# A recurrent layer and a gated convolution in one kernel: the written-out order of all queues is replaced by another order of the same operations

## The chip, the cores and the metric

The kernel runs on one core of a Trainium2 chip. The metric is the device time of one execution, in microseconds (us), smaller is better. Times are medians of several runs; a profile comes from one further, profiled execution.

## The reference, cut to what matters

The inputs `x`, `r_gate` and `i_gate` have 4 sequences of 6336 steps with 256 channels each, in fp32. First comes a gated linear recurrence along each sequence:

```
log_a = 8 * sigmoid(r_gate) * log(clip(sigmoid(a_param), 1e-6, 1 - 1e-6))
a     = exp(log_a)
u     = sqrt(max(1 - a*a, 1e-6)) * sigmoid(i_gate) * x
h[t]  = a[t] * h[t-1] + u[t];   y[t] = h[t]          # per sequence and channel
```

Then comes a gated unit on `y`: a causal convolution of 5 taps for each channel, a sigmoid of it, and two 256x256 products:

```
gate = sigmoid(sum_k conv_w[k] * y[t-4+k])
out  = (gate * (y @ w_val)) @ w_out
```

## The kernel before, in words

The four sequences lie one behind the other as 25344 rows. They are cut into 50 load **windows** (49 of 512 rows, the last of 256), numbered w, and into 27 **chunks**, numbered c: chunk 0 is window 0, chunk 1 is window 1, chunks 2 to 24 are two windows each (chunk c is windows 2c-2 and 2c-1), chunks 25 and 26 are windows 48 and 49. On the output side the last window is two windows of 128 rows, 49 and 50. The halves of the 256 channels are h = 0 and 1.

There is no loop over the work. A string `ORDER` lists some 900 words, one for each operation, and a loop at the end of the kernel (L588) calls the function of each word. Every engine takes its own instructions in the order of the words, one after the other, and waits at its next one until that one's inputs are there and its output place is free. So the string fixes five queues at once, and the numbers behind `@` in a word say which of the eight PSUM banks it uses. The words, with engine and line of the profile:

| word | engine | what it does |
|---|---|---|
| `lr.w`, `li.w`, `lx.w` | SP, L292 | DMA load of a window of r_gate, i_gate, x (512 KB each) into rings of 4 windows |
| `st.w` | SP, L562 | DMA store of an output window (512 KB) from a ring of 4 |
| `ta.c`, `tb.c` | ACT, L310, L313 | tanh of r_gate and i_gate (frees the load's place) |
| `tr.c.h` | PE, L357 | transposes of the r part into PSUM |
| `ex.c.h` | ACT, L373 | a = exp(...) into `aring`, for two chunks at once |
| `sq.c.h`, `sa.c.h` | POOL L381, ACT L389 | a*a; the one or the other engine, by word |
| `rt.b.k` | ACT, L406 | square root, for two chunks at once; needs a table load (L578) before and behind |
| `rd.0.0` | DVE, L419 to L427 | the root of chunk 0 in eight arithmetic steps |
| `nt.c` | PE, L441 | transposes of the root into PSUM |
| `pp.w`, `up.w` | POOL, L320, L332 | (tanh + 1), and its product with x into `uring` |
| `xp.w`, `uv.w` | PE L337, DVE L346 | the same product for five windows near the start, with x passed through PSUM |
| `xg.c` | DVE, L452, L456 | product with the root |
| `xt.c.h` | PE, L466 | transposes of it into PSUM |
| `sc.c.h` | DVE, L499 | the recurrence as a scan, into `yring` |
| `cv.w` | PE, L511 | convolution, 20 products with diagonals |
| `tg.w` | ACT, L518 | tanh of it into `tgring` |
| `vl.w` | PE, L526 | y @ w_val |
| `gv.w` | DVE, L531 | gate times value |
| `ou.w.0` | PE, L541 | product with w_out |
| `cd.w.0`, `ca.w.0` | DVE L549, ACT L551 | copy from PSUM to `oring`; the one or the other engine, by word |
| `s_...` | several | set-up: identity, constants from `a_param`, the diagonals, the weights |

A chunk goes through loads, `ta`, `tr`, `ex`, `sq`, `rt` (four chunks, in two pieces, between two table loads), `nt`, `xg`, `xt`, `sc`, and then each of its windows through `cv`, `tg`, `vl`, `gv`, `ou`, a copy and `st`. A load of window w waits until the operation that read window w-4 from the same ring is through. SP issues loads and stores from one queue: a store whose copy is not done yet holds every load behind it.

Of the kernel before, what the change touches and what calls it, by code (L numbers as in the profile page):

```python
# [49 lines left out]
xt.1.1@6 xt.2.1@0 sc.1.1 tg.0 li.9 sc.2.1 li.8 ex.4.1 vl.0@4,5 xt.2.0@1 tr.4.0@6,7 tb.4 gv.0 sq.5.1 cv.1@2,3 sc.2.0  # L50
ex.4.0 li.11 pp.5 lx.7 xp.4@4,5 lx.6 pp.6 uv.4 ta.6 pp.7 nt.3@6,7 up.5 ou.0.0@0,1 ta.7 lr.14 cv.3@4,5 cd.0.0 li.10
sq.5.0 lx.9 xg.3 tg.3 cv.2@0,1 lr.15 tg.1 lx.8 st.0 vl.1@6,7 sq.4.1 tg.2 xt.3.1@4 gv.1 tb.5 tr.6.0@0,1 sc.3.1 up.7
tr.6.1@6,7 ex.6.0 vl.2@2,3 up.6 lx.11 gv.2 li.12 ou.1.0@4,5 ex.6.1 lr.17 cd.1.0 xt.3.0@2 lr.16 sq.4.0 lx.10 sc.3.0
li.13 tb.6 ou.2.0@6,7 sq.7.0 vl.3@0,1 ta.8 li.15 cv.4@4,5 gv.3 sq.6.1 cd.2.0 tg.4 lr.18 ou.3.0@2,3 cd.3.0 sq.7.1
xp.8@0,1 lx.12 uv.8 rt.3.0 li.14 vl.4@2,3 st.1 sq.6.0 gv.4 lr.19 xp.9@6,7 uv.9 pp.11 lx.13 ou.4.0@2,3 rt.3.1 pp.10
cd.4.0 st.2 nt.4@6,7 up.10 xg.4 nt.5@0,1 xg.5 xt.4.0@4 up.11 lx.14 sc.4.0 xt.5.0@3 nt.6@6,7 tb.7 xt.4.1@2 sc.4.1
vl.5@0,1 ta.9 cv.5@4,5 li.16 pp.12 pp.13 xg.6 tg.5 lr.21 up.12 lr.20 tb.8 gv.5 li.17 tr.8.0@6,7 lx.15 sc.5.0 xt.6.1@0
up.13 lx.16 ex.8.0 xt.5.1@1 li.18 li.19 tr.8.1@4,5 sc.5.1 nt.7@2,3 pp.14 ex.8.1 st.3 ou.5.0@6,7 sq.9.0 st.4 ta.10 xg.7
cv.8@4,5 lx.17 up.14 cd.5.0 cv.6@2,3 tg.8 sc.6.1 xt.6.0@1 tg.6 pp.15 vl.6@4,5 ta.11 cv.7@2,3 sq.8.1 gv.6 cv.9@6,7 tg.7
lr.24 sc.6.0 up.15 lr.25 tb.9 st.5 ou.6.0@2,3 lr.23 tr.10.0@4,5 sq.8.0 cd.6.0 tg.9 vl.7@0,1 ex.10.0 st.6 gv.7 vl.8@2,3  # L60
lx.19 pp.16 xt.7.1@6 li.20 gv.8 xt.7.0@7 sq.9.1 tb.10 tr.10.1@0,1 sc.7.1 ou.7.0@4,5 sq.11.0 ex.10.1 cv.10@2,3 li.23
cd.7.0 tg.10 cv.11@0,1 sq.11.1 sc.7.0 st.7 ta.13 lr.22 lx.18 ou.8.0@4,5 li.21 pp.17 li.22 vl.9@2,3 tg.11 cd.8.0 sq.10.1
lr.29 gv.9 vl.11@4,5 sq.10.0 st.8 rt.4.0 gv.11 vl.10@0,1 ou.9.0@6,7 gv.10 up.17 cd.9.0 ou.10.0@0,1 rt.4.1 cd.10.0 up.16
ou.11.0@6,7 cd.11.0 st.10 nt.8@2,3 lr.28 pp.19 lx.21 xg.8 nt.9@0,1 lx.20 pp.18 xg.9 xt.8.1@3 cv.12@6,7 up.18 sc.8.1
ta.12 xt.8.0@5 up.19 tg.12 lr.26 sc.8.0 nt.10@2,3 lr.27 tb.11 st.9 tr.12.1@6,7 xt.9.1@1 xg.10 cv.14@4,5 ex.12.1 li.24
pp.20 li.25 sc.9.1 lx.22 pp.21 vl.14@2,3 lx.23 tg.14 cv.13@6,7 sq.13.1 tb.12 gv.14 vl.12@4,5 up.21 gv.12 tg.13
# [43 lines left out]
def kernel(  # L110
# [80 lines left out]
    with tc.manual_schedule():  # L191
# [187 lines left out]
        def op_sq(c, h):  # L379
            e, a = squares(c, h)  # L380
            nc.gpsimd.tensor_tensor(out=e, in0=a, in1=a, op=ALU.mult)  # L381
# [228 lines left out]
```

## Time and profile before

| what | value |
|---|---|
| median of 3 runs | 281.95 us (281.42 to 282.34) |
| profiled execution, span from the first to the last instruction | 279.6 us |
| around the span (median less span) | 2.4 us |
| PE, DVE, ACT, POOL busy | 243.8, 258.2, 267.0, 233.0 us |
| moved by DMA | 104.75 MB, 375 GB/s on average |

The profiled execution has no time of its own beside its span; the median of the runs less that span, 2.4 us, is taken for what lies around it.

How to read the profile: a row of the view of groups names the line, the engine, the operation, output and inputs, the shape and the count, then the busy time, the mean of one in ns, and the engine's idle time just ahead of these instructions with what ended it. A row of the timeline gives start and duration in us; `x2` behind it are two instructions that follow each other. A row of the view of windows gives, for a stretch of time, its length, the busy time and count of instructions of each engine, the clock that TensorE was granted (1.00 is full), the busy share of the 16 DMA engines and the rate at which they moved data. A row of the view of waits gives the total, the number and the longest of the waits of one line for another.

### The profile page before, as it was taken

How to read it: one execution, taken by the hardware profiler on the slowest of the kernel's cores; microseconds unless marked ns; L12 is line 12 of the kernel's file. 1: busy time of each engine (PE TensorE's matmuls, PEld its weight loads, DVE VectorE, ACT ScalarE, POOL GpSimd, SP SyncE). 2: the span in 40 equal slices, each digit the busy share in tenths (PEclk: the TensorE clock that was granted, in tenths of full speed). 3: DMA queues.
4: the chain of work that ended last, by engine and by line, in shares of the span. 5: the costliest groups of instructions: out<-in, count | busy, mean ns of one | idle time of the engine just before them, and what ended most of it. 6: DMA issues, size and time to landing. Idle time of an engine off the chain costs nothing. (4 is left out here: it accounts for less than half of the span.)

```text
span 279.6 us, 6233 instructions
## 1 busy us (share of the span) xinstructions
PE 243.8 (87%) x2493; PEld 164.9 (59%) x2493; DVE 258.2 (92%) x221; ACT 267.0 (96%) x187; POOL 233.0 (83%) x152
## 2 busy tenths in 40 slices
PE   2368999898799779999889999899999899999994
PEld 2143566456647466874566575666675756856563
DVE  5587797899999999899999999999999999999992
ACT  5999999999999999999999999999999999999754
POOL 1569679997999998999999999999999977984200
PEclk9998899999999999999999999999999999999999
DMA  7999999999999999999999999999999999742765
GB/s 275 411 405 385 388 409 409 413 409 409 419 408 417 415 414 416 413 416 409 420 413 341 415 420 414 414 411 420 416 363 407 420 378 400 286 176 92 283 263 194
DMA packets 29563, 104.75 MB, mean 375 GB/s; under 512 B 3287, under 2 KB 4062, under 8 KB 29534
## 3 DMA queue, kind: packets, MB, share of 16 engines
q1 hardware_dynamic: 29520, 104.35, 94.4%
q8 instruction: 19, 0.31, 0.4%
q14 instruction: 10, 0.08, 0.1%
q10 hardware_dynamic: 14, 0.01, 0.0%
HBM read 78.39 MB, written 25.95 MB: 373 GB/s over the span
## 5 line engine op out<-in xcount | busy, mean ns | idle before, releaser
L381 POOL TENSOR_TENSOR ering<-aring 128x1024 f32<-128x1024 f32 (+1 forms) x51 | 90.7, 1799 | 13.8 <-ACT aring L373 13.7
L332 POOL TENSOR_TENSOR uring<-tbring,xring 128x1024 bf16<-128x1024 bf16 (+1 forms) x45 | 95.5, 2139 | 3.2 <-DMA xring<-in_x_dram 1.7
L499 DVE TENSOR_TENSOR_SCAN yring<-aring,yring,banks 128x1024 bf16<-128x1024 f32 (+4 forms) x46 | 96.8, 2116 | 0.8 <-PE banks L466 0.7
L511 PE MATMUL banks<-yring,diag 64*64 64x512 bf16 (+6 forms) x1080 | 63.1, 362 | 3.8 <-ACT aring L373 1.1
L531 DVE SCALAR_TENSOR_TENSOR tgring<-tgring,banks 128x1024 bf16<-128x1024 bf16 (+1 forms) x51 | 59.4, 1178 | 6.1 <-PE banks L526 5.1
L320 POOL TENSOR_SCALAR tbring<-tbring 128x1024 bf16<-128x1024 bf16 (+1 forms) x45 | 46.3, 1040 | 10.3 <-ACT tbring L313 10.3
L541 PE MATMUL banks<-wo,tgring 128*128 128x256 bf16 x396 | 50.9, 273 | 4.4 <-DVE tgring L531 2.1
L373 ACT ACTIVATE aring<-banks,khf 128x2048 f32<-128x2048 bf16 (+3 forms) x32 | 52.9, 1689 | 0.2 <-PE banks L357 0.2
L526 PE MATMUL banks<-yring,wv 128*128 128x512 bf16 (+4 forms) x216 | 50.1, 361 | 2.7 <-DVE oring L549 1.0
L518 ACT ACTIVATE tgring<-banks 128x1024 bf16<-128x1024 f32 (+1 forms) x51 | 50.6, 1011 | 0.8 <-PE banks L511 0.6
L541 PEld LDWEIGHTS <-tgring 128*128 128x128 bf16 x396 | 42.3, 114 | 14.2 <-DVE tgring L531 5.8
L310 ACT ACTIVATE taring<-rring 128x2048 bf16<-128x2048 f32 (+2 forms) x27 | 47.9, 1785 | 1.7 <-DMA rring<-in_r_gate_dram 1.7
L313 ACT ACTIVATE tbring<-iring 128x2048 bf16<-128x2048 f32 (+2 forms) x27 | 48.1, 1782 | 0.0
L511 PEld LDWEIGHTS <-diag 64*64 64x64 bf16 x1080 | 29.4, 105 | 27.7 <-issue 12.5
L406 ACT ACTIVATE ering<-ering 128x4096 bf16<-128x4096 f32 (+3 forms) x14 | 43.6, 3157 | 0.1
L549 DVE COPY oring<-banks 128x1024 f32<-128x1024 f32 (+1 forms) x34 | 39.9, 1189 | 0.4 <-PE banks L541 0.4
L357 PE MATMUL banks<-ident_b,taring 128*128 128x128 bf16 x396 | 29.4, 230 | 8.5 <-ACT taring L310 4.5
L466 PE MATMUL banks<-ident,uring 128*128 128x128 f32 x198 | 30.3, 279 | 4.4 <-DVE uring L452 1.6
L357 PEld LDWEIGHTS <-taring 128*128 128x128 bf16 x396 | 26.0, 103 | 12.3 <-issue 6.3
L526 PEld LDWEIGHTS <-wv 128*128 128x128 bf16 x216 | 19.1, 97 | 23.8 <-issue 10.2
L466 PEld LDWEIGHTS banks<-ident,uring 128*128 128x128 f32 x198 | 21.9, 141 | 14.5 <-DVE uring L452 3.4
L441 PEld LDWEIGHTS banks<-ident,ering 128*128 128x128 f32 x184 | 24.2, 208 | 6.8 <-issue 3.0
(52 smaller groups left out, 160.0 us busy)
## 6 DMA issues: line engine op xcount, KB each, us to landing
rring<-in_r_gate_dram SPq DMA_DIRECT2D x49, 512.0 KB, 8.4
iring<-in_i_gate_dram SPq DMA_DIRECT2D x49, 512.0 KB, 9.0
xring<-in_x_dram SPq DMA_DIRECT2D x49, 512.0 KB, 9.4
out_dram<-oring SPq DMA_DIRECT2D x49, 512.0 KB, 9.0
oring<-in_moe_w_val_dram SPq DMA_DIRECT2D x1, 256.0 KB, 8.9
rring<-in_r_gate_dram SPq DMA_DIRECT2D x1, 256.0 KB
iring<-in_i_gate_dram SPq DMA_DIRECT2D x1, 256.0 KB, 6.5
xring<-in_x_dram SPq DMA_DIRECT2D x1, 256.0 KB
```

The costliest lines, as they stand in the source:

```text
L313: nc.scalar.activation(**tangent(c, tbring, NTI, iring, NII))
L332: nc.gpsimd.tensor_tensor(out=u, in0=t1, in1=xt, op=ALU.mult)
L357: nc.tensor.transpose(out=bank[:, o:o + P], in_=taring[:, place(w, NTR), j, h * P:(h + 1) * P], identity=ident_b[:])
L373: nc.scalar.activation(out=dst, in_=src, func=ACT.Exp, scale=khf[:, h:h + 1], bias=khf[:, h:h + 1])
L381: nc.gpsimd.tensor_tensor(out=e, in0=a, in1=a, op=ALU.mult)
L466: nc.tensor.transpose(out=out[:, o + q:o + wins[w] // 2:nq], in_=uring[:, w % NU, q, h * P:(h + 1) * P, :].rearrange("p d two -> p (d two) ...
L499: nc.vector.tensor_tensor_scan(out=yring[:, h, col:col + o1 - o0], data0=aring[:, h, a_at[c] + o0:a_at[c] + o1], data1=xT[:, o0:o1], initi ...
L511: nc.tensor.matmul(out=gp[oh * 64:oh * 64 + 64, h, a:b], lhsT=diag[half * 64:half * 64 + 64, h, k, :], rhs=yring[half * 64:half * 64 + 64, ...
L518: nc.scalar.activation(out=tgring[:, w % NTG, :, 0:outs[w]], in_=live.pop(("gp", w))[:, :, 0:outs[w]], func=ACT.Tanh, scale=0.5)
L526: nc.tensor.matmul(out=val[:, m, a:b], lhsT=wv[:, hk, m * P:(m + 1) * P], rhs=yring[:, hk, col:col + b - a], start=(hk == 0), stop=(hk == ...
L531: nc.vector.scalar_tensor_tensor(out=tgring[:, w % NTG, :, 0:outs[w]], in0=tgring[:, w % NTG, :, 0:outs[w]], scalar=1.0, in1=live.pop(("va ...
L541: nc.tensor.matmul(out=ops[:, j * D:(j + 1) * D], lhsT=gv[:, hk, j:outs[w]:J], rhs=wo[:, hk, :], start=(hk == 0), stop=(hk == H - 1))
```

## The change

The string `ORDER` is another one. The functions that the words call and the rings that they use do the same as before. Counted by words, the work is the same but for these:

- The copy of window 20 moves from ACT (`ca.20.0`) to DVE (`cd.20.0`). At the end, `cd.49.0 ca.50.0` becomes `ca.49.0 cd.50.0`.
- Of the squares, `sa.21.1` on ACT becomes `sa.20.1`, and `sa.26.0` and `sa.26.1` (256 columns each) go from ACT to POOL.
- The set-up words `s_kt` and `s_diag` are split into their PE and DVE parts, `s_ktp s_ktd` and `s_dgp s_dgc s_dgd`. `op_vl` accepts a single bank for the last two short windows. Three new functions (`op_pq`, `op_uq`, `op_sb`) are called by no word.

All else is where a word stands, and its banks. The queues in the first part of the run, taken from the two strings (the first line of each pair is before, the second after):

```
DVE  rd.0.0 uv.0 xg.0 sc.0.0 sc.0.1 xg.1 uv.2 sc.1.0 xg.2 sc.1.1 sc.2.1 gv.0 sc.2.0 uv.4 cd.0 xg.3 gv.1 sc.3.1 gv.2 cd.1 sc.3.0 gv.3 cd.2 cd.3 uv.8 gv.4 uv.9 cd.4 xg.4 xg.5
DVE  rd.0.0 uv.0 xg.0 uv.2 sc.0.0 sc.0.1 xg.1 sc.1.0 xg.2 sc.1.1 sc.2.0 uv.4 sc.2.1 gv.0 xg.3 cd.0 gv.2 gv.1 sc.3.1 cd.2 sc.3.0 gv.3 cd.1 cd.3 gv.4 uv.9 uv.8 cd.4 xg.4 xg.5

PE   tr.2.1 tr.2.0 xp.0 nt.0 xt.0.0 nt.1 xt.0.1 xp.2 nt.2 xt.1.0 cv.0 tr.4.1 xt.1.1 xt.2.1 vl.0 xt.2.0 tr.4.0 cv.1 xp.4 nt.3 ou.0.0
PE   tr.2.1 tr.2.0 xp.0 nt.0 xp.2 xt.0.0 xt.0.1 nt.1 xt.1.0 nt.2 xt.1.1 cv.0 xt.2.0 tr.4.1 xp.4 tr.4.0 xt.2.1 vl.0 cv.1 nt.3 cv.2 ou.0.0

ACT  ta.6 ta.7 tg.3 tg.1 tg.2 tb.5 ex.6.0 ex.6.1 tb.6 ta.8 tg.4 rt.3.0 rt.3.1 tb.7 ta.9 tg.5
ACT  tg.1 tb.4 tg.2 ta.6 ta.7 tg.3 tb.5 ex.6.1 ex.6.0 tb.6 tg.4 rt.3.0 rt.3.1 tb.7 tg.5 ta.8 ta.9

SP   lx.7 lx.6 lr.14 li.10 lx.9 lr.15 lx.8 st.0 lx.11 li.12 lr.17 lr.16 lx.10 li.13 li.15 lr.18 lx.12 li.14 st.1 lr.19 lx.13 st.2
SP   lx.7 li.9 li.8 lx.6 st.0 li.10 li.11 lr.16 lx.9 st.2 lx.8 lx.10 st.1 li.12 li.13 st.3 lr.15 lr.14 lx.11 st.4 lr.17
```

Two further places, DVE around chunk 8 and the end of SP's queue:

```
DVE  cd.9 cd.10 cd.11 xg.8 xg.9 sc.8.1 sc.8.0 xg.10
DVE  cd.11 cd.9 xg.8 sc.8.1 xg.9 sc.8.0 sc.9.1

SP   li.49 li.48 st.37 lx.47 lx.48 st.38 st.40 lx.49 st.39 st.42 ...
SP   li.49 lx.46 st.37 lx.48 li.48 lx.49 lx.47 st.39 st.38 st.40 ...
```

Of the diff itself, the head and the end of the string and the code that changes:

```diff
-s_ident s_small s_kt s_diag lr.1 lr.0 lr.2 lr.3 li.0 ta.1 lr.5 tr.1.1@3 ta.0 tr.1.0@1 ex.1.0 lr.4 tr.0.1@2 li.1 ex.0.1
+s_ident s_small lr.1 lr.0 s_wl.3 lr.3 s_ktp s_ktd lr.2 s_dgp ta.1 s_dgc tr.1.0@2 lr.5 s_dgd ta.0 tr.1.1@7 ex.1.0
...
-ca.48.0 cv.50@0,1 gv.49 vl.50@2,3 tg.50 st.48 ou.49.0@6 gv.50 cd.49.0 ou.50.0@7 st.49 ca.50.0 st.50
+vl.50@6 vl.49@7 gv.50 tg.49 st.48 ou.50.0@1 gv.49 cd.50.0 ou.49.0@2 st.50 ca.49.0 st.49
...
-        def s_kt():
-
+        def s_ktp():
             kps = banks[:, 0]
             nc.tensor.transpose(out=kps[:, 0:H], in_=ap2[0:H, :], identity=ident[0:H, 0:H])
+
+        def s_ktd():
+            kps = banks[:, 0]
...
-        def op_vl(w, at, _):
-            val = banks[:, at:at + 2]
+        def op_vl(w, *at):
+            val = banks[:, at[0]:at[0] + 2] if len(at) == 2 else banks[:, at[0]].rearrange("p (h n) -> p h n", h=H)
+            assert len(at) == 2 or outs[w] <= 256
```

More of the change, by code (lines that the diff above doesn't have):

```diff
@@ L50 @@
[L50 to L54, printed above, removed]
@@ L249, in s_kt, with s_dgp @@
                                     op0=ALU.max, op1=ALU.min)
-        def s_diag():
+        def s_dgp():
             wps = banks[:, 1]
@@ L332, in op_up, with op_pq, op_uq @@
             nc.gpsimd.tensor_tensor(out=u, in0=t1, in1=xt, op=ALU.mult)
+        def op_pq(c):
+            w, k = cwins[c][0], len(cwins[c])
+            t = tbring[:, place(w, NTI):place(w, NTI) + k, 0:wins[w] // P, :].rearrange("p k j d -> p (k j d)")
+            nc.gpsimd.tensor_scalar(out=t, in0=t, scalar1=1.0, scalar2=1.0, op0=ALU.mult, op1=ALU.add)
+        def op_uq(c):
+            w, k = cwins[c][0], len(cwins[c])
+            nc.gpsimd.tensor_tensor(
+                out=uring[:, w % NU:w % NU + k].rearrange("p k q d two -> p (k q) two d"),
+                in0=tbring[:, place(w, NTI):place(w, NTI) + k].rearrange("p k (q two) d -> p (k q) two d", two=2),
+                in1=xring[:, w % NX:w % NX + k].rearrange("p k (q two) d -> p (k q) two d", two=2), op=ALU.mult)
         def op_xp(w, *at):
```

127 lines of the change are left out of this document (70 added, 57 removed).

## The prediction, made before the run

> **What bounds the kernel now.** I read the page's busy shares and slices first, then the view of windows cut at the places where the pace changes.
>
> ```profile
> PE 243.8 (87%) x2493; PEld 164.9 (59%) x2493; DVE 258.2 (92%) x221; ACT 267.0 (96%) x187; POOL 233.0 (83%) x152
> ...
> DMA  7999999999999999999999999999999999742765
> ```
>
> ```profile
> 20.30:42.00 21.70, 19.30 (x134) 11.39 (x133) 17.12 (x18) 21.64 (x13) 17.51 (x15) 0.92 1.03 394
> 42.00:63.80 21.80, 19.40 (x173) 12.49 (x172) 19.18 (x18) 21.59 (x14) 21.65 (x13) 1.00 1.03 410
> 63.80:266.00 202.20, 187.40 (x2025) 128.77 (x2025) 200.73 (x152) 199.97 (x140) 184.79 (x113) 1.00 0.96 380
> 266.00:272.00 6.00, 6.00 (x53) 3.79 (x51) 5.57 (x8) 3.82 (x4) 0.00 (x0) 1.00 0.61 240
> ```
>
> Four things are near their limits at once, but they don't bind alike. ACT has the largest busy share; before the tail it hardly pauses, and the difference to the window's length is mostly the step from one instruction to the next. DVE is what the end hangs on: from 63.8 to 266 us it works 200.73 of 202.20 us, so only 1.47 us are idle, and from 266 to 272 another 0.43. Ahead of that it is starved: 4.58 us idle from 20.3 to 42 and 2.62 from 42 to 63.8, 7.2 in all. The DMA row is full up to the 34th slice, so loads are a limit of nearly the same height. The tail shows what follows the last scan:
>
> ```profile
> 270.48 1.39 DVE L499 TENSOR_TENSOR_SCAN yring<-aring,yring,uring 128x256 bf16<-128x256 f32 x2
> ...
> 276.53 0.37 ACT L551 COPY oring<-banks 128x256 f32<-128x256 f32 x1 [0.98 <-PE banks L541]
> ```
>
> The last scan ends at 271.87, the last copy at 276.90, and the span at 279.6. In the new order the same operations follow the last scan, with windows 49 and 50 exchanged. I take these 7.7 us as unchanged (0.5 either way). So the question is when DVE ends its last scan: its start, plus its work, plus its idle time.
>
> **The change part by part.**
>
> *Work moved between engines.*
>
> ```profile
> L549 DVE COPY oring<-banks 128x1024 f32<-128x1024 f32 x33 | 39.4, 1213 | 0.4 <-PE banks L541 0.4
> L551 ACT COPY oring<-banks 128x1024 f32<-128x1024 f32 x16 | 16.4, 1025 | 4.3 <-PE banks L541 4.3
> L389 ACT ACTIVATE ering<-aring 128x256 f32<-128x256 f32 x2 | 0.9, 438 | 0.0
> L381 POOL TENSOR_TENSOR ering<-aring 128x512 f32<-128x512 f32 x6 | 6.2, 1041 | 7.6 <-ACT aring L373 7.6
> ```
>
> The copy of window 20 leaves ACT (-1.0 us) and goes to DVE, where nothing covers it in a queue with 1.47 us of slack in 202: **+1.2 us** on the path. If the new order left DVE waiting elsewhere the copy could slip into such a wait, so its bounds are 0 and 1.2; I take 1.2. The two small squares leave ACT (-0.9) for POOL, two instructions that this trace shows only at 512 columns (1.04 each); at 256 columns they lie between nothing and 1.04, some 0.6 each by halving. POOL is the idlest of the four, and they end ahead of the last root. `sa.20.1` for `sa.21.1` and the exchange of the last two copies cost nothing: same shapes, same engines. The split of the set-up words moves DVE instructions under 1 us that wait for the first loads anyway. ACT thus gets 1.9 us shorter, which I count at nothing, because ACT then waits for what DVE makes.
>
> *The start, 20.3 to 63.8 us.* Here I walked both queues by hand. Up to `xg.4` both orders give DVE the same set of operations, so the difference is idle time alone.
>
> ```profile
> 19.12 1.22 DVE L427 SCALAR_TENSOR_TENSOR ering<-ering,banks 128x1024 bf16<-128x1024 f32 x1
> 21.32 0.74 DVE L346 SCALAR_TENSOR_TENSOR uring<-tbring,banks 128x512 bf16<-128x512 bf16 x1 [0.98 <-PE banks L337]
> 23.03 0.73 DVE L346 SCALAR_TENSOR_TENSOR uring<-tbring,banks 128x512 bf16<-128x512 bf16 x1 [0.96 <-PE banks L337]
> ...
> 28.35 0.74 DVE L346 SCALAR_TENSOR_TENSOR uring<-tbring,banks 128x512 bf16<-128x512 bf16 x1 [0.34 <-PE banks L337]
> 29.98 0.76 DVE L346 SCALAR_TENSOR_TENSOR uring<-tbring,banks 128x512 bf16<-128x512 bf16 x1 [0.90 <-PE banks L337]
> ...
> 42.52 1.23 DVE L549 COPY oring<-banks 128x1024 f32<-128x1024 f32 x1 [0.36 <-PE banks L541]
> ...
> 46.16 1.22 DVE L531 SCALAR_TENSOR_TENSOR tgring<-tgring,banks 128x1024 bf16<-128x1024 bf16 x1 [1.25 <-PE banks L526]
> ```
>
> ```profile
> 19.21 3.78 PE L337 MATMUL banks<-xring,ident 128*128 128x512 f32 x4 [2.39 <-ACT aring L373]
> ...
> 26.27 3.68 PE L337 MATMUL banks<-xring,ident 128*128 128x512 f32 x4
> ...
> 38.68 1.99 PE L337 MATMUL banks<-xring,ident 128*128 128x512 f32 x4 [0.51 <-DVE tgring L531]
> ```
>
> `rd.0.0` ends at 20.3 and `uv.0` waits for the two halves of `xp.0`. That stays: `xp.0` still stands behind `tr.2.0`, which now waits for `ex.2.1`, at most 0.2 earlier. What changes is `xp.2`. Before it starts at 26.27 and takes 3.68; a later `xp` takes 1.99. After, it follows `nt.0` at about 23.4. Which duration it has is read from the clock:
>
> ```profile
> 19.60:23.00 3.40, 3.40 (x6) 1.23 (x5) 1.48 (x2) 3.38 (x3) 3.40 (x3) 1.00 1.04 396
> 23.00:26.40 3.40, 2.04 (x13) 1.38 (x13) 2.74 (x5) 3.39 (x3) 3.40 (x2) 1.00 1.03 364
> 26.40:29.80 3.40, 3.40 (x5) 1.21 (x6) 2.34 (x3) 3.38 (x2) 3.32 (x3) 0.50 1.06 402
> ```
>
> A stretch in which PE was busy throughout (3.40 of 3.40) is followed by one at full clock, the one with 2.04 of 3.40 by one at half. The new `xp.2` would fall into the full stretch, 23.4 to 25.3, and fill it to about 3.1 of 3.4 with the four `xt.0` and `nt.1` that follow. Bounds 1.99 and 3.68; I take 1.99. (The Trainium skill, TensorE: Matmul & The Clock Gate, Part 1, says that the clock follows a window of activity of 3413 ns, with which these rows agree, but also that this window runs freely and that the same kernel then shows different numbers of slow matmuls. By that rule the saving may be gone in some executions; the sum would then be that of the last rival.)
>
> With that, DVE's waits up to `xg.4` are: 0.8 and 1.15 in `uv.0`, 0.1 in `uv.2`, 0.55 ahead of `sc.1.0` (its `xt.1.0` starts when `xg.1`, right ahead, ends), 0.25 ahead of `sc.2.1`, 1.0 ahead of `cd.0` (`ou.0.0` stands behind `nt.3` and `cv.2`), 1.4 ahead of `cd.3` (`ou.3.0` needs the banks that `cd.1`, right ahead, reads), and three of 0.1. That is 5.6 against 7.2: **-1.6 us**. The bounds: nothing gained, and 2.6, if the 1.0 at `cd.0` were hidden too. ACT allows it: `ta.8` moves behind the root, so `rt.3.0`, which started at 58.43, can start up to 1.9 earlier.
>
> ```profile
> 54.27 1.94 ACT L310 ACTIVATE taring<-rring 128x2048 bf16<-128x2048 f32 x1
> ...
> 58.43 7.13 ACT L406 ACTIVATE ering<-ering 128x4096 bf16<-128x4096 f32 x2
> ```
>
> *The middle and the tail, 63.8 to 272 us.* Before there are 1.9 us of idle DVE (1.47 + 0.43). In the new order I looked for pairs on DVE with PE between them and nothing to fill the gap: one is left, `xg.8` right ahead of `sc.8.1`, some 0.65 (in the walk's `sc.1.0` it is 0.55). With 0.4 for the tail and 0.25 for the rest I count 1.3: **-0.6 us**. The bounds are -1.3 (only the one pair) and several us above zero, since PE, POOL and the loads all stand in new places; the rivals price that.
>
> Sum against the profiled execution: -1.6 + 1.2 - 0.6 = -1.0, a span of 278.6. The median stands 2.4 above the span, so **280.9 us**.
>
> **The rivals.**
>
> *The loads set the pace.* For it: the DMA row is full, and the few waits for loads show that these come just in time.
>
> ```profile
> ACT taring L310 <- DMA rring<-in_r_gate_dram: 1.7, 3, 1.3
> ...
> POOL uring L332 <- DMA xring<-in_x_dram: 1.7, 3, 0.7
> ```
>
> An engine that is 1.6 us ahead at 64 us waits for its loads until the lead is gone. The saving of the start is then lost, and of the 1.2 of the copy most disappears into such waits: 282.1 us. Against it: DVE itself, packed for 200 us, shows no such wait.
>
> *Stores ahead of loads drain the queue (the slower side).* SP's order puts stores earlier:
>
> ```profile
> 46.08 0.34 SPq L562 DMA_DIRECT2D out_dram<-oring  x1
> 49.61 0.33 SPq L292 DMA_DIRECT2D xring<-in_x_dram  x1
> ...
> 60.08 0.37 SPq L562 DMA_DIRECT2D out_dram<-oring  x1
> ```
>
> Up to `st.0` (46.08 before), the old order had issued 38 loads and the weights, the new one has 32 and the weights, 17.3 MB. From issue to landing the first load took 3.6 us, of which its 0.52 MB at 0.41 MB per us are 1.3, so data flow some 1.7 behind an issue's end:
>
> ```profile
> 0.72 1.88 SPq L292 DMA_DIRECT2D rring<-in_r_gate_dram  x4
> ...
> 4.31 1.06 ACT L310 ACTIVATE taring<-rring 128x1024 bf16<-128x1024 f32 x1 [1.29 <-DMA rring<-in_r_gate_dram]
> ```
>
> From about 2.5 on, 17.3 MB at 0.41 are through at about 45. `st.0` waits for `cd.0`, which ends at 43.75 before; with `xg.3` now ahead of it at 45.0, if no lead was won, and its data flow at 46.7: dry for some 1.8. Then `st.2`, which now stands ahead of `lx.8` and `lx.10`:
>
> ```profile
> 52.14 2.34 DVE L499 TENSOR_TENSOR_SCAN yring<-aring,yring,banks 128x1024 bf16<-128x1024 f32 x1
> 55.08 1.22 DVE L531 SCALAR_TENSOR_TENSOR tgring<-tgring,banks 128x1024 bf16<-128x1024 bf16 x1 [0.60 <-PE banks L526]
> 56.22 2.47 DVE L549 COPY oring<-banks 128x1024 f32<-128x1024 f32 x2
> ```
>
> 2.6 MB have been added, through at 53. `cd.2` ended at 57.4; moved ahead of `cd.1`, `sc.3.0` and `gv.3` (1.2, 2.3 and 1.2) it ends at 52.7, and its data flow at 54.5: dry for 1.5. With the lead of the walk these are some 0.5 together; without it 3.3. And before has dry places that the new order loses:
>
> ```profile
> 199.50:203.00 3.50, 3.50 (x38) 2.49 (x40) 3.50 (x3) 3.50 (x4) 3.50 (x3) 1.00 1.03 421
> 203.00:206.50 3.50, 3.50 (x52) 3.06 (x45) 3.50 (x4) 3.50 (x4) 3.50 (x2) 1.00 0.98 360
> 206.50:210.00 3.50, 3.15 (x37) 1.75 (x35) 3.41 (x3) 3.50 (x2) 3.50 (x3) 1.00 1.02 355
> ```
>
> 7 us at 358 in place of 421 is 1.0 lost. So 3.3 - 1.0 - 0.4 (the little that loads come ahead of need) = +1.9: 283.8 us. It decides from the point at which loads of the middle arrive later than their readers are free.
>
> *The clock falls back at `xp.2`.* Then `sc.0.0` is 1.7 later, and the sum is +0.7: 282.6 us.
>
> *No new waits at all in the middle.* Then -1.6 + 1.2 - 1.9 = -2.3: 279.6 us.
>
> **How the numbers follow.** A difference under 0.3% (0.85 us, so 281.1 to 282.8) is about what a measurement of this kernel cannot tell from none. Forecast 0.40, of which about 0.05 reaches over 281.1; loads set the pace 0.18; stores drain the queue 0.29, with the price between 282.8 and 285; clock 0.05; no new waits 0.08. That makes 0.43 faster, 0.28 same, 0.29 slower. The range is 279.4 to 284.0: about a tenth lies below and a tenth above. The forecast's own range is 280.1 to 281.6.
>
> **What would show it right or wrong.** Right: DVE idle between the end of `rd.0.0` and `xg.4` near 5.6 us, `xp.2` near 2 us, `xg.4` near 62.2 in place of 63.8; from there to the last scan at most 1.3 idle; DMA full up to about 238. Wrong: a clock of 0.5 behind 23 us, rates under 350 GB/s between 42 and 60, ACT or POOL waiting for loads by more than the 1.7 us each of before, or waits of DVE behind 64 us that add up to over 2. A DVE that is packed and still ends later would say that the operations themselves got longer, which I have left out.

## The result: 288.69 us in place of 281.92

The changed kernel takes 288.69 us (median of 4 runs, 287.40 to 290.06), the kernel before 281.92 beside it (281.42 to 282.34): a ratio of 1.0244, 95% interval 1.0209 to 1.0278. The prediction said 280.9, and its range ended at 284.0. The profiled execution of the changed kernel has a span of 287.2 us; before it was 279.6. These two lie 7.6 us apart, the medians 6.8; the sums from the traces below add up to the 7.6. (The profiled execution of the changed kernel took 288.98 us, so 1.8 us lie around its span. The 2.4 that the prediction added hold some 0.6 more, probably because the profiled execution of before was shorter than the median.)

The same operations stand on other lines now: a load on L299, `up` on L339, `xg` on L477, `xt` on L491, `sc` on L524, `tg` on L543, `vl` on L552, `gv` on L557, `ou` on L567, `cd` on L575, `st` on L588. In the experiments, those on the kernel before included, each of these is one line less.

The page of the changed kernel, busy time and the slices of 7.2 us:

```profile
PE 244.2 (85%) x2493; PEld 164.8 (57%) x2493; DVE 260.0 (91%) x222; ACT 267.6 (93%) x184; POOL 234.1 (82%) x154
...
DMA  6999999999999999999999999999999999941716
GB/s 232 408 413 410 382 409 327 398 351 416 414 371 343 414 418 411 410 412 394 408 379 404 411 403 411 419 393 417 408 415 419 412 353 361 359 185 75 292 76 257
```

The engines work nearly as long as before (DVE 1.8 us more, of which 1.2 are the copy), so the time went into waits. The DMA row, still all nines, hides what the GB/s row shows: 327 in the slice of 43 to 50 us, 351 in that of 57 to 65, 371 and 343 from 79 to 93. The windows of the changed kernel say where DVE waited, in two answers (the row from 23 us shows the clock at the new place of `xp.2`):

```profile
20.30:42.00 21.70, 18.58 (x132) 11.15 (x134) 17.67 (x18) 20.68 (x13) 18.02 (x14) 0.92 1.03 400
42.00:63.80 21.80, 19.96 (x175) 12.43 (x175) 19.01 (x16) 21.77 (x13) 21.06 (x13) 1.00 0.96 359
63.80:84.00 20.20, 15.80 (x160) 11.46 (x163) 18.09 (x12) 17.73 (x12) 13.16 (x9) 0.92 1.02 410
```

```profile
23.00:26.40 3.40, 2.98 (x14) 1.73 (x13) 3.08 (x6) 3.37 (x4) 3.40 (x3) 1.00 1.02 407
...
63.80:278.90 215.10, 194.32 (x2075) 132.53 (x2075) 207.96 (x158) 205.65 (x141) 186.73 (x116) 0.99 0.94 369
```

And the window from 63.8 to 84 us in the kernel before:

```profile
63.80:84.00 20.20, 17.03 (x197) 11.78 (x197) 20.20 (x15) 20.17 (x14) 18.67 (x12) 1.00 1.03 411
```

The last scan ends at 278.9, 7.0 us later than before. The sum: DVE reaches `xg.4` 0.6 later (64.39 for 63.8). From there to the last scan it works 1.8 longer, of which the copy is 1.2. The rest probably comes with the waits: two scans in a row take 4.58 us and a single one 2.34, so an operation behind a wait loses the 0.1 by which neighbours overlap. And it is idle for 6.55 us (215.10 less 207.96, less the 0.59 ahead of `xg.4`) in place of 1.90, that is 4.65 more. Behind the last scan come another 0.6.

The window from 63.8 to 84 us is the largest piece of the idle time: 2.11, where it was nothing. Of that, 0.59 is the wait ahead of `xg.4`, 0.64 a wait of `xg.6` for POOL and 0.88 a wait of `gv.6` for PE. The other 5.0 of the 7.14 are spread over small waits up to the last scan.

Two things meet in that window behind `xg.4`. First the loads. SP's queue in the timeline of the changed kernel (L588 is a store, L299 a load):

```profile
38.38 0.33 SPq L299 DMA_DIRECT2D xring<-in_x_dram  x1
45.52 0.35 SPq L588 DMA_DIRECT2D out_dram<-oring  x1
...
48.35 0.38 SPq L299 DMA_DIRECT2D xring<-in_x_dram  x1
51.27 0.34 SPq L588 DMA_DIRECT2D out_dram<-oring  x1
51.71 1.40 SPq L299 DMA_DIRECT2D xring<-in_x_dram  x2
55.77 0.34 SPq L588 DMA_DIRECT2D out_dram<-oring  x1
...
58.12 0.34 SPq L588 DMA_DIRECT2D out_dram<-oring  x1
...
59.67 0.47 SPq L299 DMA_DIRECT2D xring<-in_x_dram  x1
```

SP stands still from 38.7 to 45.5 for `st.0`, then for `st.2` and `st.1`; `lx.11` is issued at 59.7, behind `st.3`. POOL, which needs it, and its waits for loads in all:

```profile
64.05 2.16 POOL L339 TENSOR_TENSOR uring<-tbring,xring 128x1024 bf16<-128x1024 bf16 x1
70.88 2.14 POOL L339 TENSOR_TENSOR uring<-tbring,xring 128x1024 bf16<-128x1024 bf16 x1 [4.67 <-DMA xring<-in_x_dram]
```

```profile
POOL uring L339 <- DMA xring<-in_x_dram: 9.1, 5, 4.7
...
ACT taring L317 <- DMA rring<-in_r_gate_dram: 3.8, 4, 1.5
```

Second a PSUM bank. PE and DVE at the same time, still in the changed kernel:

```profile
67.64 1.28 PE L536 MATMUL banks<-yring,diag 64*64 64x512 bf16 x20
72.47 0.66 PE L491 MATMUL banks<-ident,uring 128*128 128x128 f32 x4 [3.55 <-DVE tgring L557]
73.06 1.50 PE L536 MATMUL banks<-yring,diag 64*64 64x512 bf16 x20
...
75.40 1.91 PE L552 MATMUL banks<-yring,wv 128*128 128x512 bf16 x4
```

```profile
71.22 1.20 DVE L557 SCALAR_TENSOR_TENSOR tgring<-tgring,banks 128x1024 bf16<-128x1024 bf16 x1
73.06 1.23 DVE L477 TENSOR_TENSOR uring<-banks,uring 128x2048 bf16<-128x2048 bf16 x1 [0.64 <-POOL uring L339]
...
77.42 1.22 DVE L557 SCALAR_TENSOR_TENSOR tgring<-tgring,banks 128x1024 bf16<-128x1024 bf16 x1 [0.88 <-PE banks L552]
```

`xt.5.0` (72.47) has had its data since 66.7, but the new string puts it in bank 3, which `vl.5` filled and `gv.5` reads until 72.4. PE, which works in order, is idle for 3.55 us, and `cv.6`, `vl.6` and `gv.6` follow late. The view of windows in stretches of 3.4 us shows a second price of the wait:

```profile
70.60:74.00 3.40, 1.53 (x24) 0.91 (x24) 2.76 (x3) 1.85 (x2) 3.12 (x3) 1.00 1.03 419
74.00:77.40 3.40, 3.40 (x18) 1.82 (x11) 2.54 (x2) 3.40 (x3) 1.20 (x3) 0.50 1.03 413
```

Behind the stretch in which PE worked for 1.53 of 3.40 us the granted clock is 0.50, and `vl.6` takes 1.91 where a `vl` takes 1.0. (The Trainium skill, TensorE: Matmul & The Clock Gate, section "A second HAM failure mode: psum-queue depth-cycling", tells of a kernel that cycles through the PSUM banks, in which PE idles briefly between groups of matmuls so often that the clock falls and rises again and again. These rows show one fall behind one long wait for a bank, 3.55 us, and not that repeated pattern.)

### The profile page after: what moved, and what is told of

It is laid out like the page before. It is cut to its first block, busy times and chain, and to the rows that moved or that the text cites. A ratio compares the mean times of both kernels' runs of the same rounds, so it can differ in the third digit from the quotient of the medians.

```text
span 287.2 us, 6240 instructions
## 1 busy us (share of the span) xinstructions
PE 244.2 (85%) x2493; PEld 164.8 (57%) x2493; DVE 260.0 (91%) x222; ACT 267.6 (93%) x184; POOL 234.1 (82%) x154
## 5 line engine op out<-in xcount | busy, mean ns | idle before, releaser
L339 POOL TENSOR_TENSOR uring<-tbring,xring 128x1024 bf16<-128x1024 bf16 (+1 forms) x45 | 95.7, 2136 | 10.9 <-DMA xring<-in_x_dram 9.1
L400 POOL TENSOR_TENSOR ering<-aring 128x1024 f32<-128x1024 f32 (+2 forms) x53 | 91.7, 1753 | 9.6 <-ACT aring L392 9.6
L524 DVE TENSOR_TENSOR_SCAN yring<-aring,yring,banks 128x1024 bf16<-128x1024 f32 (+4 forms) x46 | 97.0, 2119 | 2.4 <-PE banks L491 2.2
L557 DVE SCALAR_TENSOR_TENSOR tgring<-tgring,banks 128x1024 bf16<-128x1024 bf16 (+1 forms) x51 | 59.2, 1180 | 5.8 <-PE banks L552 4.3
L543 ACT ACTIVATE tgring<-banks 128x1024 bf16<-128x1024 f32 (+1 forms) x51 | 50.6, 998 | 6.0 <-PE banks L536 5.8
L567 PE MATMUL banks<-wo,tgring 128*128 128x256 bf16 x396 | 51.2, 274 | 5.6 <-DVE tgring L557 2.9
L552 PE MATMUL banks<-yring,wv 128*128 128x512 bf16 (+4 forms) x216 | 50.3, 366 | 1.9 <-ACT aring L392 1.4
L567 PEld LDWEIGHTS <-tgring 128*128 128x128 bf16 x396 | 41.6, 114 | 17.0 <-DVE tgring L557 7.9
L575 DVE COPY oring<-banks 128x1024 f32<-128x1024 f32 (+1 forms) x35 | 41.5, 1192 | 2.7 <-PE banks L567 2.4
L536 PEld LDWEIGHTS <-diag 64*64 64x64 bf16 x1080 | 28.6, 106 | 25.3 <-issue 10.4
L491 PE MATMUL banks<-ident,uring 128*128 128x128 f32 x198 | 31.4, 284 | 10.4 <-DVE uring L477 3.9
L491 PEld LDWEIGHTS banks<-ident,uring 128*128 128x128 f32 x198 | 22.7, 144 | 20.5 <-DVE uring L477 6.3
L552 PEld LDWEIGHTS <-wv 128*128 128x128 bf16 x216 | 19.5, 98 | 21.7 <-issue 7.6
L466 PE MATMUL banks<-ident,ering 128*128 128x128 f32 x184 | 27.6, 295 | 4.6 <-ACT ering L431 3.5
```

The source lines that it names most:

```text
L339: nc.gpsimd.tensor_tensor(out=u, in0=t1, in1=xt, op=ALU.mult)
L491: nc.tensor.transpose(out=out[:, o + q:o + wins[w] // 2:nq], in_=uring[:, w % NU, q, h * P:(h + 1) * P, :].rearrange("p d two -> p (d two) ...
L524: nc.vector.tensor_tensor_scan(out=yring[:, h, col:col + o1 - o0], data0=aring[:, h, a_at[c] + o0:a_at[c] + o1], data1=xT[:, o0:o1], initi ...
L536: nc.tensor.matmul(out=gp[oh * 64:oh * 64 + 64, h, a:b], lhsT=diag[half * 64:half * 64 + 64, h, k, :], rhs=yring[half * 64:half * 64 + 64, ...
L543: nc.scalar.activation(out=tgring[:, w % NTG, :, 0:outs[w]], in_=live.pop(("gp", w))[:, :, 0:outs[w]], func=ACT.Tanh, scale=0.5)
L552: nc.tensor.matmul(out=val[:, m, a:b], lhsT=wv[:, hk, m * P:(m + 1) * P], rhs=yring[:, hk, col:col + b - a], start=(hk == 0), stop=(hk == ...
```

## The experiments

Theory 1: loads behind stores that wait for their copies. Theory 2: the new neighbours and banks on PE, DVE and ACT. In all runs the mixed queues were put into one string in which each word stands behind those that it depends on.

### One whole queue exchanged: e1, e2, e5, e6

e1 is the changed kernel with SP's queue of before:

```diff
-SP of the changed kernel: ... lx.6 st.0 li.10 li.11 lr.16 lx.9 st.2 lx.8 lx.10 st.1 ...
+SP of the kernel before:  ... lx.6 lr.14 li.10 lx.9 lr.15 lx.8 st.0 lx.11 li.12 lr.17 ...
```

> The changed kernel with SP's queue alone put back to the order of before; PE, DVE, ACT and POOL keep the new order. Theory 1 (the new SP order holds loads behind stores, DMA runs below its rate between 42 and 64 us and again behind 79, and POOL, ACT and then DVE wait for loads): DVE's idle time from 63.8 us to the last scan goes from 7.0 to about 2, so some 282.5 to 284 us; POOL waits for x by under 3 us in place of 9.1. Theory 2 (the waits come from the new neighbours on PE, DVE and ACT, whatever the loads do): 287 to 289 us. Theory 3 (old SP order does not fit the new compute order, each alone is fine): over 289.

Measured: 328.55 us, 1.165 (1.162 to 1.169).

e2 is the kernel before with SP's queue of the changed one (the same two lines the other way round).

> The kernel before with SP's queue alone in the new order (three short stretches of it, st.10 and st.11 past lr.24, st.33 to st.35 past lr.48 and lx.44, had to be swapped, since the old compute order needs those loads earlier). Theory 1: 286 to 288 us, with DVE waiting in the stretch 63.8 to 84, where it did not wait before. Theory 2: 281.5 to 283.

Measured: 397.51 us, 1.412 (1.409 to 1.416).

e5 keeps the changed kernel's sequence of loads and moves its stores back:

```diff
-lx.6 st.0 li.10 li.11 lr.16 lx.9 st.2 lx.8 lx.10 st.1 li.12 li.13 st.3
+lx.6 li.10 li.11 lr.16 lx.9 lx.8 lx.10 st.0 li.12 li.13 lr.15 lr.14 lx.11
```

> The changed kernel; SP keeps the new order of the loads, but each store moves behind as many loads as the store of the same rank has ahead of it in the old order (5 to 19 loads further for most stores up to st.19). PE, DVE, ACT and POOL keep the new order. Theory 1 (stores that wait for their copies hold loads, DMA runs below its rate, POOL and ACT and then DVE wait): 282.5 to 285 us, DVE idle from 63.8 us to the last scan 2 to 4 in place of 7.0, the rate between 42 and 64 us near 400 GB/s in place of 359. Theory 2 (the new neighbours on PE, DVE and ACT make the waits): 287 to 289.

Measured: 304.87 us, 1.083 (1.078 to 1.089).

e6 moves the stores of the kernel before forward:

```diff
-lx.7 lx.6 lr.14 li.10 lx.9 lr.15 lx.8 st.0 lx.11 li.12
+lx.7 st.0 lx.6 lr.14 li.10 lx.9 st.1 lr.15 lx.8 st.2
```

> The kernel before; SP keeps its old order of the loads, but each store comes as early, counted in loads ahead of it, as the store of the same rank in the new order. Theory 1: 285 to 290 us (SP held at st.0 until 43.8 with lx.6 behind it, which is needed at 49.5). Theory 2: 281.5 to 283.

Measured: 350.02 us, 1.235 (1.225 to 1.245).

They lie 40, 116, 16 and 68 us above the kernel whose compute queues they keep. e1 came out as its third outcome, the other three outside all of theirs. What follows is that SP's queue and the compute queues are made for each other. In e2 and e6 stores ahead of their copies hold the queue: SP waits 165.7 and 126.2 us in all for copies on DVE. In e1 and e5 it is the other way round: SP waits 65.8 and 36.4 us for a `ta` to free a load's place, and copies on DVE wait 22.8 and 18.0 us for late stores. None of the four tells the theories apart; the exchange itself is what they price.

### The string's halves: e3, e4, and a control: e7

e3 has all queues as before up to `xg.4` and as changed from there; e4 the other way round. e7 has the queues of before in another sequence of words.

```
e3: all five queues of before up to xg.4 (SP up to st.2), then the rest in the changed order
e4: all five queues as changed up to xg.4 (SP up to lr.17), then the rest in the order of before
```

> All five queues in the old order up to xg.4 (SP up to st.2), from there in the new order. It holds the copy of window 20 on DVE. Theory 1, with the damage done in the start (SP dry between 42 and 64, lx.11 late): 283 to 284.5 us, since the idle 0.6 of the start and the 2.1 of 63.8 to 84 go. Theory 1 with the damage in the later stores (st.5, st.7, st.18): 285.5 to 287. Theory 2: 286 to 288.

> All five queues in the new order up to xg.4 (SP up to lr.17), from there in the old order; the copy of window 20 stays on ACT. Theory 1 with the damage in the start: 284 to 285.5 us (0.6 at xg.4, 2.1 from 63.8 to 84). Damage in the later part alone: 282 to 283.

> All five queues and all banks as in the kernel before, but the words of the string in another sequence that gives the same queues (and the set-up words split as in the changed kernel). Both theories: 281.4 to 282.4 us. If it is not the same, the sequence of the words matters beside the queues, and the mixed orders have to be read with that.

Measured: e3 287.88 (ratio 1.0186 to 1.0230), e4 287.81 (1.0191 to 1.0234), e7 281.36 (0.997 to 1.0005). The queues alone count, not the text. e3 lies in the range of theory 2, e4 above both of its ranges. The two halves don't add up: each costs 6, both together 7. The windows of e4, and its waits:

```profile
42.00:63.80 21.80, 19.92 (x174) 12.70 (x177) 18.76 (x18) 21.77 (x13) 21.07 (x14) 1.00 0.96 354
63.80:84.00 20.20, 13.56 (x118) 11.03 (x121) 15.40 (x11) 16.22 (x10) 12.66 (x9) 0.83 1.00 394
```

```profile
POOL uring L338 <- DMA xring<-in_x_dram: 7.9, 4, 3.7
```

The start of the changed order leaves the loads behind (354 GB/s from 42 to 63.8, as there), and the order of before then pays 4.80 us of idle DVE up to 84; at the last scan it is 5.9 late. In e3 SP stands 10.9 us ahead of `st.5` and DVE is idle for 3.6 in the same window. Each seam has a debt of its own, so the two runs show that the damage can arise early, not how much of it does.

### The loads at the start: e9, and the whole of SP's queue: e10, e11

e9 changes 20 words of SP's queue and nothing else:

```diff
-li.9 li.8 lx.6 st.0 li.10 li.11 lr.16 lx.9 st.2 lx.8 lx.10 st.1 li.12 li.13 st.3 lr.15 lr.14 lx.11 st.4 lr.17
+lx.6 li.9 li.8 lx.9 lx.8 li.10 li.11 st.0 lr.15 lr.14 lx.11 lr.16 li.12 lx.10 li.13 lr.17 st.1 st.2 st.3 st.4
```

> The changed kernel; in SP's queue only the 20 words from li.9 to lr.17 stand in another sequence, worked out from the changed kernel's own trace: each load at the time at which its place was free there, loads that are needed sooner first, and no load behind a store whose copy is not done (lx.8, lx.9, li.10, li.11 ahead of st.0; lr.14, lr.15, lx.11, lx.10 ahead of st.1 to st.4). Nothing else is changed. Theory 1, loads held behind st.0 to st.4 are the cause of the idle DVE from 63.8 to 84 us: the rate from 42 to 63.8 us rises from 359 to about 400 GB/s, POOL's waits for x fall from 9.1 to under 4, DVE's idle time from 63.8 to 84 from 2.1 to under 0.5: 285.5 to 287 us. Theory 2 (neighbours on the compute engines): 288.3 to 289.

Measured: 286.62 us (1.0147 to 1.0204), 2.1 under the changed kernel. The windows of e9, and DVE's timeline at `gv.6`:

```profile
42.00:63.80 21.80, 20.80 (x183) 13.36 (x176) 19.00 (x17) 21.77 (x13) 21.00 (x13) 1.00 1.03 411
63.80:84.00 20.20, 15.91 (x148) 10.90 (x146) 17.38 (x12) 17.18 (x12) 14.50 (x9) 0.83 0.88 351
```

```profile
77.68 1.22 DVE L556 SCALAR_TENSOR_TENSOR tgring<-tgring,banks 128x1024 bf16<-128x1024 bf16 x1 [2.75 <-PE banks L551]
```

And PE at `xt.5.0`:

```profile
71.43 1.11 PE L490 MATMUL banks<-ident,uring 128*128 128x128 f32 x4 [3.48 <-DVE tgring L556]
```

The time lies in the range of theory 1, but the reason given for it fell. The rate is repaired, 411 for 359, and `up.11` no longer waits; POOL's waits for x fall from 9.1 to 4.4. Yet DVE is idle for 2.82 us in the window, more than the 2.11 of the changed kernel: it comes to `gv.6` earlier and waits there for `vl.6`, which is late by the bank, for `xt.5.0` still waits 3.48 us for `gv.5`. (e3, with the loads of before at the start and the banks of the changed order, waits at the same place: 2.58 us ahead of `gv.6`.) From `xg.4` to the last scan DVE is idle for 6.38 us in place of 6.55, so nearly all that the profiled execution gains lies ahead of `xg.4` (63.34 for 64.39). Theory 1 alone is refuted for this window.

e10 works out all of SP's queue from `li.9` on in that way, e11 does the same to the kernel before.

```diff
-e10: ... lr.17 li.14 li.15 lx.12 lx.14 lx.13 lr.18 lr.19 li.17 lr.20 lr.21 st.5 li.16 lx.15 ...
+e10: ... lr.17 li.14 li.15 st.1 st.2 lx.12 lx.13 st.3 st.4 lx.14 li.17 li.16 lr.18 lr.19 lx.15 ...
-e11: ... li.9 li.8 li.11 lx.7 lx.6 lr.14 li.10 lx.9 lr.15 lx.8 st.0 lx.11 ...
+e11: ... li.9 li.8 lx.7 lx.6 li.11 li.10 lr.14 lr.15 lx.8 lx.9 st.0 li.12 lx.11 ...
```

> As the run before, but the whole of SP's queue from li.9 on is worked out anew from the changed kernel's trace. Theory 1: 283.5 to 285.5 us, since the later waits for loads go too. Theory 2: the remaining waits stay, 286 to 288.5. A third outcome: the new queue does not fit the moments at which places come free once DVE runs earlier, and it is slower, over 289.

> The kernel before with SP's queue from li.9 on worked out in the same way from its own trace. DVE has hardly a wait there that a load could take away, so 281.2 to 282.5 us; if it is clearly slower, the way in which the queue is worked out costs time by itself, and the two runs on the changed kernel have to be read with that.

Measured: e10 287.15 (1.0154 to 1.0254), e11 284.31 (1.0073 to 1.0120). By e11 the way of working out a whole queue costs 2.7 by itself; so e10, no better than e9, says nothing on the later loads.

### The bank: e13, and the bank with the loads: e14

e13 changes four banks, e14 has these and the 20 words of e9.

```diff
-xt.5.0@3   vl.6@0,1   tr.8.1@2,3   ou.5.0@0,1
+xt.5.0@1   vl.6@2,3   tr.8.1@0,1   ou.5.0@2,3
```

> The changed kernel with four banks changed: xt.5.0 in bank 1 in place of 3, vl.6 in 2,3 in place of 0,1, tr.8.1 in 0,1 in place of 2,3, ou.5.0 in 2,3 in place of 0,1; all five queues as they are. xt.5.0 then waits for sc.4.0 (ended 69.1) and not for gv.5 (72.4). Theory 2 (here the choice of banks is what makes DVE idle from 63.8 to 84): cv.6 starts near 71.4 in place of 73.1, the wait ahead of gv.6 (0.9) goes: 287 to 288 us, since the late lx.11 (xg.6 waits 0.6) stays. Theory 1 (loads alone): 288.3 to 289.

> The four banks of e13 together with the 20 words of SP's queue of e9. If loads and banks are two separate causes of the idle time from 63.8 to 84, both have to go before DVE gains: DVE idle there falls from 2.8 (e9) to under 0.8, and 284 to 285.3 us. If the banks are of no account: 286.4 to 287, as in e9.

Measured: e13 288.28 us (1.0192 to 1.0256), not to be told from the changed kernel; e14 **284.00** (1.0057 to 1.0121), 4.7 under it. The windows of e14, in three answers, then PE and DVE:

```profile
63.80:84.00 20.20, 16.64 (x192) 11.42 (x193) 20.20 (x14) 20.17 (x14) 16.38 (x11) 1.00 1.00 396
```

```profile
70.60:74.00 3.40, 2.26 (x24) 1.34 (x25) 3.40 (x4) 3.40 (x3) 0.62 (x1) 1.00 1.04 417
74.00:77.40 3.40, 3.40 (x47) 3.12 (x44) 3.40 (x3) 3.40 (x3) 3.17 (x2) 1.00 1.02 407
```

```profile
63.80:274.10 210.30, 191.22 (x2048) 131.32 (x2068) 207.19 (x158) 204.78 (x141) 186.94 (x116) 1.00 0.94 373
```

```profile
68.47 0.66 PE L490 MATMUL banks<-ident,uring 128*128 128x128 f32 x4
```

```profile
75.07 1.20 DVE L556 SCALAR_TENSOR_TENSOR tgring<-tgring,banks 128x1024 bf16<-128x1024 bf16 x1
```

`xt.5.0` runs at 68.47 in place of 72.47, the stretch from 74 has the full clock (PE worked for 2.26 of 3.40 us ahead of it, in place of 1.53), `gv.6` at 75.07 follows without a wait, and DVE is not idle at all from 63.8 to 84. Between `xg.4` and the last scan it is idle for 3.1 us; the changed kernel has 6.55, e9 6.4 and e13 6.1. So the loads and the bank are two causes that stand side by side: taken away alone they leave that idle time nearly as it is, together they halve it. In the medians they give 2.1 and 0.4 alone (the latter within the spread) and 4.7 of the 6.8 together. In e13 DVE's wait only moves, to 1.4 us ahead of `cd.7.0`.

Not all of the 4.7 need be these waits. Four of e14's six runs had a mean clock of 0.992 to 0.994, and no run of the changed kernel, e9 or e13 was above 0.986. At 0.981 and 0.982 e14 took 286.24 and 285.05 us, the changed kernel 287.40 and 288.40: some 2.3 of the 4.7 are there at the same clock. Whether the mended queues raise the clock or these four runs were lucky is not shown. Nor do the stretches give the point at which the clock falls: in e13 PE works for 1.63 of 3.40 us from 70.6 on, and the next stretch still has 1.00.

### The pair, the copy, and all together: e8, e12, e15, e16, e17, e18

e8 and e12 are the copy of window 20 by itself:

```diff
-e8 (changed kernel): cd.20.0
+e8 (changed kernel): ca.20.0
-e12 (kernel before): ca.20.0
+e12 (kernel before): cd.20.0
```

> The changed kernel with the copy of window 20 back on ACT, at its place in the string. If the copy stands on the path as the prediction costed it: 287.5 us (1.2 less). If DVE waits for something else behind it anyway: 288.3 to 288.7. If ACT has no room there: 288.7 to 289.7.

> The kernel before with the copy of window 20 on DVE in place of ACT, at the same place of the string. If the prediction's price holds: 282.9 us (1.2 more). If it slips into a wait or gives ACT room that DVE uses: 281.5 to 282.3.

Measured: e8 287.96 (1.0164 to 1.0251), not to be told from the changed kernel; e12 282.25 (1.0006 to 1.0037), that is 0.65 (0.2 to 1.0) more than before: half of the 1.2, and within the second of its outcomes.

e15 undoes the pair of which the prediction spoke:

```diff
-DVE cd.9 xg.8 sc.8.1 xg.9    PE nt.8 cv.12 xt.8.1 nt.9
+DVE cd.9 xg.8 xg.9 sc.8.1    PE nt.8 nt.9 xt.8.1 cv.12
```

> The changed kernel with xg.9 ahead of sc.8.1 on DVE, and on PE nt.9 and xt.8.1 ahead of cv.12, as in the kernel before; banks and other queues as they are. The prediction put this pair at 0.65; the trace shows 0.8 of idle DVE ahead of sc.8.1: 287.9 us. If what follows waits for ACT or PE anyway: 288.4 to 289.

Measured: 288.76 (1.0204 to 1.0287), nothing gained. DVE and POOL in e15:

```profile
108.38 1.23 DVE L476 TENSOR_TENSOR uring<-banks,uring 128x2048 bf16<-128x2048 bf16 x1 [1.63 <-POOL uring L338]
```

```profile
104.09 4.26 POOL L338 TENSOR_TENSOR uring<-tbring,xring 128x1024 bf16<-128x1024 bf16 x2
```

`xg.9` cannot start earlier, since `up.16` on POOL ends at 108.35. So the scan loses nothing by its place ahead of `xg.9`: with the two exchanged, DVE waits for POOL instead.

e16 is e14 with the pair of e15 and the copy of e8; e17 is e14 with the copy of e8 alone; e18 is e17 with PE's tail mended:

```diff
-e18 PE: cv.48 ou.46.0 vl.48 ou.47.0 cv.50 ou.48.0 cv.49 vl.50 vl.49
+e18 PE: cv.48 vl.48 ou.46.0 ou.47.0 cv.50 ou.48.0 vl.50 cv.49 vl.49
```

> All four together: SP's 20 words of e9, the four banks of e13, the pair of e15, the copy of window 20 back on ACT. If the terms add: 288.7 less 2.1, 1.5, 0.8 and 0.7, so 283 to 284 us, and the rest up to 281.7 is the many small waits of DVE for PE. If they overlap: 284.5 to 286.

> The kernel of e14 (four banks, 20 words of SP's queue) with the copy of window 20 back on ACT. From e12, where it costs 0.65 in the kernel before, and e8, where its return gives 0.7: 283.3 us. If ACT has no room there (it is the fullest engine): 284 to 285.

> As e17, and on PE vl.48 ahead of ou.46.0 and vl.50 ahead of cv.49, so that gv.48 follows the last scan at once and gv.50 waits less: from the last scan's end to the last copy 5.0 us as in the kernel before, in place of 5.6. 0.3 to 0.6 under e17, so 282.7 to 283 us. If the last copies wait for something else: as e17.

Measured: e16 287.66 (1.0172 to 1.0229), e17 286.48 (1.0138 to 1.0187), e18 286.60 (1.0164 to 1.0203). With the copy back on ACT all three are 2.5 us or more above e14. e16 and e17 are misses, and e18 is no better than e17, as its second outcome had it. The timelines of DVE and PE in e17 show where some of that is:

```profile
164.61 1.23 DVE L574 COPY oring<-banks 128x1024 f32<-128x1024 f32 x1 [1.74 <-ACT tgring L542]
```

```profile
163.48 1.03 PE L566 MATMUL banks<-wo,tgring 128*128 128x256 bf16 x8 [1.26 <-ACT tgring L542]
```

Ahead of `cd.21` DVE now waits for 1.74 us, as it does in e8, e16 and e18 too. This is a bank once more: `ou.21` (163.48) goes into banks 6 and 7, which `tg.22` reads, and on ACT the copy of window 20 stands ahead of `tg.22`. In e14 that copy is on DVE, two words ahead of `cd.21`, which then follows without a wait. So in the new order the copy fills time in which DVE would wait, and on ACT it is in the way: from the start of `xg.14` to that of `cd.21` e17 takes 5.33 us, e14 4.64.

The 2.5 us between e17 and e14 are more than the copy. Four of e17's six runs had a mean clock of 0.980 or 0.981, only two of e14's. At 0.992 and 0.993 e17 took 285.53 and 284.94 us, 1.4 above e14's four runs there. e18's tail is not shorter either (ahead of `gv.50` DVE waits 2.4 for 2.0).

What holds the remaining 2.2 us of e14 above the kernel before (284.00 for 281.77 beside it) is not settled by a run. Its profile shows the last scan 2.3 later than before, for the copy's 1.2 and 1.2 more of idle time (3.1 for 1.90), and another 0.5 behind it. No version ran that beats the kernel before by more than the noise.

## Why the prediction was wrong, point by point

- *The bound* was right: DVE's busy time hardly moved, and the end follows its idle time.
- *The start, -1.6*: wrong, +0.6 in the profiled execution. From the end of `rd.0.0` to `xg.4` DVE is idle for 7.4 us, not 5.6. `xp.2` ran from 23.4 to 25.3 at full clock (1.00 in the row above), and the waits at `cd.0` (0.9 for 1.0) and `cd.3` (1.1 for 1.4) were as walked. But I walked PE and DVE and took ACT as given. Its rows in the changed kernel, with DVE's for `xg.2` and `xg.4`:

```profile
25.08 4.57 ACT L431 ACTIVATE ering<-ering 128x1024 bf16<-128x1024 f32 x2
```

```profile
54.40 1.92 ACT L320 ACTIVATE tbring<-iring 128x2048 bf16<-128x2048 f32 x1
...
58.55 7.13 ACT L431 ACTIVATE ering<-ering 128x4096 bf16<-128x4096 f32 x2
```

```profile
31.79 1.22 DVE L477 TENSOR_TENSOR uring<-banks,uring 128x2048 bf16<-128x2048 bf16 x1 [1.06 <-PE banks L466]
```

```profile
64.39 2.36 DVE L477 TENSOR_TENSOR uring<-banks,uring 128x2048 bf16<-128x2048 bf16 x2 [0.66 <-PE banks L466]
```

  `rt.2.0` ends at 29.65, and `xg.2` waits 1.06 where nothing was counted. `rt.3.0` starts at 58.55 and not "up to 1.9 earlier": `tb.6` stands at 54.40, where `ta.8` stood before, so ACT had already lost what the move of `ta.8` gave. `xg.4` waits 0.66 for that root. These two waits, 1.7 together, are nearly all that the walk lacked. The walk also took the end of `rd.0.0`, 20.3, as fixed. Here it is 20.83 (its last instruction, on L452 now, starts at 19.61), and why is not settled. The +0.6 itself is that of one execution: in e8, e13 and e15, whose queues are the same up to there, `xg.4` starts at 63.88, 63.87 and 63.63, about where it was before. In none of them is the saving of 1.6.
- *The copy, +1.2*: 0.65 by itself in the kernel before; in the new order its return to ACT gives nothing that can be told (e8) or costs about 1.4 at the same clock (e17). The bound "0, if it slips into a wait" was the better value there.
- *The middle, -0.6*: this is the step that failed, by 5.3 us: "one pair is left", 1.3 us of idle DVE from `xg.4` to the last scan. It is 6.55, so +4.65 against the 1.90 of before. Of these, 3.4 go when the bank and the loads are mended together (e14); where the other 1.2 come from is open. I looked for pairs on DVE with PE between them. I did not look at the banks behind `@`, each of which is a wait of PE for the reader of what stood there before, and I priced the late loads apart from it. The pair I named is there (0.8), but exchanging it gains nothing, since `up.16` is late: it ends at 108.9, in the kernel before at 103.0.
- *The tail, unchanged within 0.5*: 8.3 for 7.7, a little outside. Ahead of `gv.50` DVE waits 1.97, and before its longest wait there was 1.45. DVE in the changed kernel:

```profile
277.51 1.39 DVE L524 TENSOR_TENSOR_SCAN yring<-aring,yring,uring 128x256 bf16<-128x256 f32 x2
...
282.32 0.42 DVE L557 SCALAR_TENSOR_TENSOR tgring<-tgring,banks 128x256 bf16<-128x256 bf16 x1 [1.97 <-PE banks L552]
```

- *The rivals*: "stores ahead of loads drain the queue" had the place (`st.0`, `st.2`) and the sign, and named the signs that came: rates near or under 350 GB/s, POOL and ACT waiting for loads by more than 1.7. Its price of +1.9 is close to the 2.1 that taking it away alone gives, but that is luck in the main: e9's trace has nearly the same idle time of DVE behind `xg.4`. And it ended at 283.8, since it counted no other wait in the middle. "The clock falls back" was put at `xp.2`, where it did not fall; it fell at 74 us, behind the bank's wait. (Where the prediction points from the clock to the sum of "the last rival", it means this one, 282.6.)

## What to carry to other kernels

Where a written-out order fixes all queues, read every bank and every ring place as a wait for its last reader, and walk all engines with them, ACT and SP too; a walk over the bound engine alone finds only the waits that its own neighbours make. When two delays run side by side, mending either shows little: before a cause is dropped because its removal gave 0.4, it is to be removed together with the other. Look at the waits as well as at the time: the medians alone would have given the loads 2.1 us that the trace doesn't show behind `xg.4`. An order of one queue can cost far more than it gains beside queues that it was not made for (e1, e2: 40 and 116 us).

## What the runs showed of the hardware that was not expected

The same kernel ran at different granted clocks, and where DVE has no cover this shows in the time. The six runs of e14: with a mean clock of 0.992 to 0.994 they took 283.53, 283.71, 283.81 and 284.19 us; with 0.981 and 0.982 they took 286.24 and 285.05. One stretch of 3.4 us at half clock lowers the mean over 283 us by 0.006 (half of 3.4 by 283). By this estimate the two slower runs had two more such stretches, and they took 1 to 2.5 us longer; only one of the six has a trace. e17 and e18, whose queues differ in PE's tail alone, were profiled at 0.980 and 0.992. From 145.8 to 149.2 us e17 has a clock of 0.61 and e18 of 1.00, and DVE is idle for 7.1 and 5.0 us from `xg.4` to the last scan. Which makes which, the wait or the low clock, is not shown.

The kernel before doesn't feel it: runs at 0.987 and at 1.000 took 282.07 and 281.34 to 282.11. (The Trainium skill, TensorE: Matmul & The Clock Gate, Part 1, says that the window runs freely, so that the same kernel measures different numbers of slow matmuls, and puts the price of the ramp under 1% of a typical span. The 1 to 2.5 of 284 us here, 0.4 to 0.9%, are of that size; that they come from the ramp no run shows.) That the changed kernel's own runs spread over 2.7 us, and those of before over 0.9, fits this. Its four runs, at 0.974 to 0.985, don't show it by themselves, but for the slowest (290.06), which had the lowest clock.
